# Attention and a low-rank mixer on one core: first batch reordered, two groups' turn of u moved to transfers, bias rows issued one head earlier

## The chip, the cores and the metric

The kernel runs on one core of a Trainium2 chip. The metric is device time in microseconds (us), from runs of the whole kernel; lower is better. A profiled execution gives a trace of every instruction of the five engines (PE is TensorE, DVE is VectorE, ACT is ScalarE, POOL is GpSimd, SP is SyncE) and of the DMA queues. PE's weight loads are a track of their own, PEld.

## What is computed

Two parts follow each other. The first is causal attention with a bias per position, for 8 batches of 8 heads, 576 positions and head size 64. The second takes the heads side by side as x (8 x 576 x 512), mixes the positions with a rank-32 product, and runs a feed-forward layer of width 2048.

```python
scores = scale * np.matmul(q, k.transpose(0, 1, 3, 2))
cum = np.cumsum(np.maximum(s, 0.0), axis=-1)
bias = -(cum[:, :, :, None] - cum[:, :, None, :])
scores = np.where(causal, -1e9, scores + np.minimum(bias, 0.0))
attn = softmax(scores)                       # along the last axis
x = (attn @ v).transpose(0, 2, 1, 3).reshape(B, S, H * D)
...
h = x.transpose(0, 2, 1) @ U @ V             # U: 576 x 32, V: 32 x 576
u = x + h.transpose(0, 2, 1)
out = u + np.maximum(u @ w_ch1, 0.0) @ w_ch2
```

## The kernel before

**Groups.** The batches go through in five groups, `GROUPS = [(0,), (1,), (2, 3), (4, 5), (6, 7)]` (L22). The first two groups share the activation tiles of one pair of batches: batch 0 is tiles 0 to 3, batch 1 tiles 5 to 8, and tile 4 (`TAIL`) holds the last 64 rows of both. A group of two batches has nine tiles of 128 rows (`TILES`, L24). The work of a group is its *front*, attention and then the mixer, and its *back*, the feed-forward layer.

**Front.** A pair of heads of one group has a number n, 0 to 19; n = 8 to 11 belong to group 2, 12 to 15 to group 3, 16 to 19 to group 4. For a head, `scores` (L455) multiplies keys by queries in four steps, each into a PSUM bank of tag "s" (three banks), and ACT writes exp of it to `pT` (L473). `weigh` (L501) multiplies these weights by v, which carries a column of ones for the sum, and DVE divides (L519, L523) into `x_sb`. Keys and queries must stand with the head dimension on the partitions. For groups 0 and 1 `turn_six` (L431) does that with six TensorE transposes and two copies of 64 x 576 (L451). For n from 8 on, POOL casts them to DRAM (`cast`, L190) and `turn_kq` (L208) brings them back with four transposing DMAs of SP's queue (L217), one per batch and tensor, 1152 rows of 128 each. Four extra rows per pair, 64 to 67 of `kT` and `qT`, hold the bias split into parts: `bias_rows` (L347) loads them from DRAM on SP's queue (L353). A transposing DMA writes all 128 partitions, so the bias rows of a pair have to wait until the transposes of that pair have landed. `kT` and `qT` have room for four pairs (`RING`). SP issues its DMAs in order, the outputs among them (L783, L787).

At the end of pair n of a front, `attention` issues on SP `bias_rows(n + 1)` for n above 10 and `turn_kq(n + 2)` for n above 9 (L639 to L642); for earlier pairs a table `late` does it (L634).

`mix` (L700) then forms `ux`, the product with U over all tiles (L708), copies it (L713), and for each tile multiplies by V (L736) and adds to x in place on DVE (L740). u must also stand with its 512 columns on the partitions, as `uT`, for the feed-forward layer. The inner function `turn` does that for two tiles at a time: eight TensorE transposes into a "pv" bank (L723) and one DVE copy (L728).

**Back.** `ffn` (L751) has two phases. In the first, for each stretch of columns in `CUTS` (L660; one stretch is a third of 1152 for the groups of two) and each of 16 slices of the width, four matmuls (L591) fill a bank "f" (three banks) and ACT takes the positive part to `hT` (L763). In the second, sixteen matmuls per tile (L768) are added to x on DVE (L779) into one of five buffers `o` and written out.

**Order of the work.** All is written out by hand. The loop at L804 runs the back of group g and steps the front of group g + 1 between its steps: both are generators that yield their cost in us, and the front is stepped as long as it is behind a ratio:

```python
ratio = FRONT[g + 1] / (BACK[g] - LEAD[g])
due, live = -LEAD[g] * ratio, True
...
due += cost * ratio
```

`LEAD[g]` is how much of the back runs before the front of the next group begins. With `FRONT` = 24.6 and `BACK` = 61.7 the front ends with the back.

**First batch.** It has no back to run beside. `first_attention` (L538) turns the keys and queries of the head pairs (`turns`, alternating keys and queries of pairs 0 to 3), runs the eight heads, and puts the weighing of a head and parts of batch 0's mixer and feed-forward between the scores. `ux_first` (L668) and `turn_first` (L678) are the mixer of batch 0; `turn_first` gets `uT` straight from a matmul with the identity plus the product with V. `begun` are three "s" banks with the first feed-forward products. `stir(n)` (L161) issues n matmuls of 128 x 128 whose result is not used.

Of the kernel before, what the change touches and what calls it, by code (L numbers as in the profile page):

```python
# [47 lines left out]
def kernel(  # L48
# [12 lines left out]
    nc = tc.nc  # L61
# [41 lines left out]
    uT = const([128, 4, 2 * S], BF16, "uT")  # L103
# [57 lines left out]
    def stir(n):  # L161


        ps = bank("pv", 2)
        for _ in range(n):
            nc.tensor.matmul(ps[:, :128], lhsT=stirrer, rhs=stirrer, start=True, stop=True)  # L166
# [261 lines left out]
        make_keep(0)  # L428


    def turn_six(g, hp, which, scalar=False):  # L431


        pb = (bank("f", 3) if g == 0 else bank("pv", 2)).bitcast(BF16)
        for hh in range(2):
            for t in range(SUB // 2):
                c = RP * (hh * (SUB // 2) + t)
                nc.tensor.transpose(
                    pb[:, c : c + RP],
                    six[g][which][:, 2 * hp + hh, 2 * D * t : 2 * D * t + 2 * D],  # L440
                    identity[:RP, :RP],
                )
        n = pairs.index((g, hp))
        to = (kT, qT)[which](n)[:D].rearrange(
            "d (h p t e) -> d h p t e", h=2, t=SUB // 2, e=2
        )
        for e in range(2):
            from_ = pb[64 * e : 64 * e + 64, : RP * SUB].rearrange(
                "d (h t p) -> d h p t", h=2, p=RP
            )  # L450
            (nc.scalar.copy if scalar else nc.vector.tensor_copy)(  # L451
                to[:, :, :, :, e], from_
            )

    def scores(kt_, qt_, p, c, tail0, first=False):  # L455

# [81 lines left out]
    def first_attention():  # L538


        turns = [(hp, which) for hp in range(4) for which in range(2)]
        for i, (hp, which) in enumerate(turns[:3]):
            turn_six(0, hp, which, scalar=i == 1)
            stir((3, 14, 34)[i])
        prepare_second()
        done, second = [], cumulate(1, 2)
        for h in range(H):
            n, hh = h // 2, h % 2
            p = next_p()
            if h == 2:  # L550
                next(second)
            quanta = scores(kT_all, qT_all, p, PW * n + S * hh, 448, True)
            next(quanta)
            next(quanta)
            if h == 7:
                ux_first((0, 1), nc.vector.tensor_copy)

            if h > 3:
                weigh(*done.pop(0))
            for _ in quanta:  # L560
                pass
            done.append((0, p, 0, h))
            if h in (3, 5, 6):
                next(second)
            if h + 3 < len(turns):
                turn_six(0, *turns[h + 3])
            if h < 5:
                stir((12, 12, 12, 12, 6)[h])
            if h == 7:
                turn_first((0, 1), 0, 256, nc.vector.tensor_copy)  # L570
            if h > 4:
                weigh(*done.pop(0))
        weigh(*done.pop(0))
        turn_first((0, 1), 256, 512, nc.scalar.copy)
        ux_first((2,), nc.vector.tensor_copy)
        begun = [bank("s", 3) for _ in range(3)]
        for nf in range(3):
            for kt in range(2):
                first_product(begun[nf], nf, kt, *CUTS[0][0])
        turn_first((2,), 0, 512, nc.scalar.copy)  # L580
        ux_first((3,), nc.vector.tensor_copy)
        for nf in range(3):
            first_product(begun[nf], nf, 2, *CUTS[0][0])
        turn_first((3,), 0, 256, nc.vector.tensor_copy)
        turn_first((3,), 256, 512, nc.scalar.copy)
        for _ in second:
            pass
        return begun
# [7 lines left out]
    def attention(g, side):  # L596

        pending = None
        turns = [(hp, which) for hp in range(4) for which in range(2)] if g == 1 else []


        for cost in (0.25, 1.8, 0.9) if turns else ():
            turn_six(g, *turns.pop(0))
            yield cost
        for hp in range(H // 2):
            n = pairs.index((g, hp))
            for hh in range(2):
                for i, bi in enumerate(SIDES[g]):
                    p = next_p()
                    quanta = scores(  # L610
                        kT_all, qT_all, p, place(n).start + (2 * i + hh) * S,
                        512 if bi == 0 else 448,
                    )
                    yield next(quanta)
                    yield next(quanta)
                    nc.vector.tensor_tensor(  # L616
                        p[:, D4:O1], p[:, D4:O1], keep[bi], ALU.min
                    )
                    if turns:
                        turn_six(g, *turns.pop(0))  # L620
                        yield 0.25
                    if pending is not None:
                        weigh(*pending)
                        yield 0.48
                    for cost in quanta:
                        yield cost
                    pending = (g, p, bi, 2 * hp + hh)
                    for _ in range(2):
                        next(side, None)
            if g == 1 and hp == 1:  # L630
                nc.vector.tensor_copy(x_sb[1][:64, TAIL, :], x_sb[0][:64, TAIL, :])


            late = {5: 8, 6: 9, 7: 10, 8: 11}  # L634
            if n - 1 in late:
                bias_rows(late[n - 1])
            if n in late:
                turn_kq(late[n])
            if n > 9:  # L639
                if n > 10:  # L640
                    bias_rows(n + 1)
                turn_kq(n + 2)  # L642
            if g == 2 and hp == 0:

                for t in (kT(11), qT(11)):
                    nc.gpsimd.tensor_copy(hold, t[:1, PW : PW + 1])
                load_group(g + 1)
            if g > 2 and hp == 1:

                c = (2 * hp) * D  # L650
                nc.gpsimd.tensor_copy(hold, x_sb[g % 2][:1, 0, c : c + 1])  # L651
                load_group(g + 1)
        weigh(*pending)
        yield 0.48
        for _ in side:
            pass
# [1 line left out]


    CUTS = [  # L660
        ((0, 256), (256, 512)),
        ((512, 832), (832, 1152)),
        *[((0, 384), (384, 768), (768, 1152))] * 3,
    ]
# [35 lines left out]
    def mix(g):  # L700

        x, tl = x_sb[g % 2], TILES[g]


        ux = bank("f", 3)
        for n, t in enumerate(tl):
            i = n % 2
            nc.tensor.matmul(  # L708
                ux[64 * i : 64 * i + 64, :], lhsT=U_cat[:, t, :64], rhs=x[:, t, :],
                start=(n == i), stop=(n + 2 >= len(tl)),  # L710
            )
        yield 0.13 * len(tl)
        nc.vector.tensor_copy(ux_sb, ux)  # L713
        if g == 1:

            nc.vector.tensor_copy(ux_sb[:32], ux0[:32])  # L716
        yield 0.65

        def turn(ns):
            pb = bank("pv", 2).bitcast(BF16).rearrange("p (d n c) -> p d n c", d=4, c=128)  # L720
            for m, n in enumerate(ns):
                for d in range(4):
                    nc.tensor.transpose(  # L723
                        pb[:, d, m, :], x[:, tl[n], 128 * d : 128 * d + 128], identity
                    )
            w = 128 * len(ns)
            c = 128 * tl[ns[0]]
            nc.vector.tensor_copy(  # L728
                uT[:, :, c : c + w],
                pb.rearrange("p d n c -> p d (n c)")[:, :, :w],  # L730
            )

        done = 0
        for n, t in enumerate(tl):
            hp_ = bank("f", 3)
            nc.tensor.matmul(  # L736
                hp_, lhsT=V_cat[:, t, :], rhs=ux_sb,
                start=True, stop=True,
            )
            nc.vector.tensor_add(x[:, t, :], x[:, t, :], hp_)  # L740
            yield 0.22
            if n >= 2 and n % 2 == 0:
                turn([done, done + 1])
                done += 2
                yield 0.45
        while done < len(tl):
            turn(list(range(done, min(done + 2, len(tl)))))
            done += 2
            yield 0.45

    def ffn(g, begun):  # L751

# [43 lines left out]

    LEAD = [5.0, 8.0, 0.0, 0.0]
    FRONT = [0.0, 17.3, 24.6, 24.6, 24.6]  # L800
    BACK = [27.4, 34.3, 61.7, 61.7, 61.7]

    begun = first_attention()
    for g in range(len(GROUPS)):  # L804
# [3 lines left out]
                pass  # L808
            break
        ahead = front(g + 1)  # L810
        ratio = FRONT[g + 1] / (BACK[g] - LEAD[g])
        due, live = -LEAD[g] * ratio, True
        for cost in back:
            due += cost * ratio
# [38 lines left out]
```

## Time and profile before

| | us |
|---|---|
| median of 3 runs | 389.03 (387.9 to 390.3) |
| the profiled execution, its own time | 388.87 |
| its span, first to last instruction | 387.2 |
| PE busy | 372.6 (96%) |
| PEld busy | 235.4 (61%) |
| ACT busy | 206.0 (53%) |
| DVE busy | 166.2 (43%) |
| POOL busy | 65.9 (17%) |

A group's line gives a duration from issue to the modelled end; matmuls overlap, so PE's cost of one is the distance between starts. "PEclk" is the clock that TensorE was granted, as a share of the full one. An instruction's line in the timeline gives in brackets how long its engine had been idle before it, and what ended that.

### The profile page before, as it was taken

What the parts mean: (1) busy time and instruction counts of PE and PEld (TensorE: products, weight loads), DVE (VectorE), ACT (ScalarE), POOL (GpSimd) and SP (SyncE); (2) the same over time, 40 slices, a digit from 0 to 9 for tenths busy, and PEclk for the clock granted to TensorE, in tenths of its full rate; (3) what the DMA queues carried; (4) which work ended last, traced back from release to release, by engine and by line L of the source; (5) the groups of instructions that cost most, each with busy time, mean ns of one, the idle gap of its engine ahead of it and who ended that gap; (6) DMA issues with size and microseconds to landing.
All of it is one profiled execution on the core that took longest, in us unless ns stands there. A gap on an engine that the chain in (4) does not pass through costs nothing.

```text
span 387.2 us, 8463 instructions
## 1 busy us (share of the span) xinstructions
PE 372.6 (96%) x3445; PEld 235.4 (61%) x3445; DVE 166.2 (43%) x385; ACT 206.0 (53%) x473; POOL 65.9 (17%) x104
## 2 busy tenths in 40 slices
PE   8899998999999979999999999999999999999995
PEld 8688865467766545666655456666655455655442
DVE  6484699551446581232243473332344471000221
ACT  4576865239977206888844007888744006773000
POOL 8784642100072200044300000000000000000000
PEclk9899999999999998999999999999999999999999
DMA  7999999999989999869991816800011110000122
GB/s 96 174 207 183 188 215 172 140 141 150 204 137 200 133 166 210 163 82 203 152 154 58 182 54 111 155 22 2 2 54 56 56 54 30 0 2 27 70 68 81
DMA packets 117989, 44.06 MB, mean 114 GB/s; under 512 B 99486, under 2 KB 113054, under 8 KB 117950
## 3 DMA queue, kind: packets, MB, share of 16 engines
q0 software_dynamic: 51376, 18.50, 44.4%
q1 hardware_dynamic: 66390, 24.99, 35.3%
q8 instruction: 27, 0.44, 0.5%
q14 instruction: 12, 0.10, 0.1%
q10 hardware_dynamic: 184, 0.03, 0.1%
HBM read 37.52 MB, written 16.97 MB: 141 GB/s over the span
## 4 chain that ended last, share of the span: by engine, by line
PE 83%; DMA 6%; DVE 5%; POOL 2%; ACT 1%; issue 1%; SPq 0%; POOLq 0%; ACTq 0%; DVEq 0%
PE ps_f L591 31%; PE ps_f L768 28%; PE ps_s L461 10%; PE ps_pv L513 8%; DMA qT<-kq_rows 3%; DMA hT<-in_k_dram 2%; PE ps_f L736 1%; PE ps_pv L723 1%; DVE qT L451 1%; DMA qT<-aug_rows 1%; POOL v_raw L229 1%; ACT pT L473 1%; POOL hT L203 1%; PE ps_f L708 1%; DVE kT L451 1%
## 5 line engine op out<-in xcount | busy, mean ns | idle before, releaser
L473 ACT ACTIVATE pT<-ps_s 128x448 bf16<-128x448 f32 (+1 forms) x256 | 120.5, 512 | 84.2 <-PE ps_s L461 81.7
L591 PE MATMUL ps_f<-uT,w 128*128 128x384 bf16 (+2 forms) x820 | 149.2, 316 | 0.0
L768 PE MATMUL ps_f<-w,hT 128*128 128x512 bf16 x576 | 147.5, 379 | 0.0
L763 ACT ACTIVATE hT<-ps_f 128x384 bf16<-128x384 f32 (+2 forms) x205 | 97.3, 476 | 54.8 <-PE ps_f L591 52.6
L591 PEld LDWEIGHTS <-w 128*128 128x128 bf16 x832 | 76.6, 98 | 35.3 <-issue 1.7
L461 PE MATMUL ps_s<-qT,kT 68*128 68x128 bf16 (+4 forms) x576 | 79.6, 242 | 4.6 <-DMA qT<-aug_rows 2.6
L768 PEld LDWEIGHTS <-hT 128*128 128x128 bf16 x576 | 52.1, 98 | 48.2 <-issue 2.4
L616 DVE TENSOR_TENSOR pT<-pT,keep 128x576 bf16<-128x576 bf16 x56 | 25.6, 456 | 108.5 <-ACT pT L473 108.2
L461 PEld LDWEIGHTS <-kT 68*128 68x128 bf16 x576 | 46.6, 98 | 35.8 <-issue 5.1
L779 DVE TENSOR_TENSOR o<-x_sb,ps_f 128x512 f32<-128x512 bf16 x36 | 24.6, 685 | 73.7 <-PE ps_f L768 71.9
L513 PEld LDWEIGHTS <-pT 128*128 128x128 bf16 x960 | 37.2, 97 | 11.7 <-DVE x_sb L528 1.7
L513 PE MATMUL ps_pv<-v_raw,pT 128*128 128x65 bf16 x960 | 40.8, 194 | 2.0 <-DVE qT L451 0.8
L229 POOL DMA_DIRECT2D v_raw<-in_v_dram x32 | 28.2, 891 | 32.6 <-PE ps_s L461 16.3
L523 DVE TENSOR_TENSOR x_sb<-ps_pv,rec 128x320 bf16<-128x320 f32 (+1 forms) x64 | 29.3, 458 | 2.2
L740 DVE TENSOR_TENSOR x_sb<-x_sb,ps_f 128x512 bf16<-128x512 bf16 x32 | 21.0, 685 | 4.7 <-PE ps_f L736 4.7
L651 POOL COPY hold<-x_sb 1x1 bf16<-1x1 bf16 x2 | 0.4, 178 | 100.4 <-DVE x_sb L523 100.4
L519 DVE RECIPROCAL rec<-ps_pv 128x5 f32<-128x5 f32 x64 | 12.2, 191 | 5.4 <-PE ps_pv L513 4.6
L166 PE MATMUL ps_pv<-hT 128*128 128x128 bf16 x141 | 12.1, 252 | 1.1 <-DVE hT L132 1.1
L728 DVE COPY uT<-ps_pv 128x1024 bf16<-128x1024 bf16 (+1 forms) x18 | 11.3, 630 | 4.3 <-PE ps_pv L723 4.0
L736 PE MATMUL ps_f<-ux_sb,V_cat 128*128 128x512 bf16 x32 | 11.8, 379 | 0.9 <-DVE ux_sb L716 0.4
L723 PEld LDWEIGHTS <-x_sb 128*128 128x128 bf16 x128 | 8.6, 98 | 5.2 <-issue 0.6
L166 PEld LDWEIGHTS <-hT 128*128 128x128 bf16 x141 | 10.5, 116 | 1.1 <-DVE hT L132 1.1
(88 smaller groups left out, 147.9 us busy)
## 6 DMA issues: line engine op xcount, KB each, us to landing
out_dram<-o SPq DMA_DIRECT2D x32, 256.0 KB
v_raw<-in_v_dram POOLq DMA_DIRECT2D x32, 128.0 KB, 17.9
w<-in_moe_w_ch_dram POOLq DMA_DIRECT2D x8, 512.0 KB, 12.5
kq_rows<-in_k_dram POOLq DMA_DIRECT2D x6, 576.0 KB, 11.1
kq_rows<-in_q_dram POOLq DMA_DIRECT2D x6, 576.0 KB, 14.5
out_dram<-o SPq DMA_DIRECT2D x8, 128.0 KB
hT<-in_k_dram POOLq DMA_DIRECT2D x4, 144.0 KB, 4.1
hT<-in_q_dram POOLq DMA_DIRECT2D x4, 144.0 KB, 4.9
```

The lines of the kernel that those rows point to most:

```text
L166: nc.tensor.matmul(ps[:, :128], lhsT=stirrer, rhs=stirrer, start=True, stop=True)
L229: nc.gpsimd.dma_start(out=dest[:, 5 * bi + t, :, :D], in_=v[b, :, 128 * t : 128 * t + 128].rearrange("h p d -> p h d"),)
L461: nc.tensor.matmul(ps[:, col : col + n], lhsT=kt_[:KA, c + kc : c + kc + 128], rhs=qt_[:KA, c + qc : c + qc + n], start=start, stop=stop,)
L473: nc.scalar.activation(p[:, at : at + n], ps[:, :n], EXP, scale=scale)
L513: nc.tensor.matmul(pv3[:, it, :], lhsT=p[:, at : at + 128], rhs=vr[:, TAIL if j == 4 else 5 * bi + j, h, :], start=(j == 0), stop=(j == it),)
L523: nc.vector.tensor_mul(x[:, 5 * bi : 5 * bi + n, h * D : h * D + D], pv3[:, :n, :D], rec[:, :n].unsqueeze(2).to_broadcast([128, n, D]),)
L591: nc.tensor.matmul(f1[:, : c1 - c0], lhsT=w1[:, kt, 128 * nf : 128 * nf + 128], rhs=uT[:, kt, c0:c1], start=(kt == 0), stop=(kt == 3),)
L616: nc.vector.tensor_tensor(p[:, D4:O1], p[:, D4:O1], keep[bi], ALU.min)
L740: nc.vector.tensor_add(x[:, t, :], x[:, t, :], hp_)
L763: nc.scalar.activation(hT[:, nf, c0:c1], f1[:, :cw], RELU)
L768: nc.tensor.matmul(f2, lhsT=hT[:, kt, 128 * t : 128 * t + 128], rhs=w2[:, kt, :], start=(kt == 0), stop=(kt == 15 and g > 0),)
L779: nc.vector.tensor_add(o, x_sb[g % 2][:, t, :], f2)
```

## The change

It has these parts.

- First batch: four turns instead of three go ahead of the heads, with 3, 14, 6 and 46 unused matmuls behind them instead of 3, 14 and 34. Within heads 0 to 4, three unused matmuls stand ahead of the third score step, and in heads 0 to 3 four more ahead of the last; the 12, 12, 12, 12 and 6 behind the heads are gone. The turns left stand behind heads 0, 1, 3 and 4 (before: 0 to 4); the last one is copied half by ACT and half by DVE. The first weighing moves from the middle of head 4 to its end.
- `CUTS[0]`: one stretch of 512 columns instead of two of 256. The three banks begun ahead of the feed-forward layer get their products with all 512 columns, three of four, before it starts.
- `turn` in `mix`, for groups 3 and 4: per tile one transposing DMA from `x_sb` to `uT` on SP's queue instead of TensorE transposes and a copy. Its cost in the interleaving is 0 instead of 0.45 per two tiles.
- `bias_rows(n + 1)` for n above 10 moves from the end of pair n to behind the first head of it.
- `LEAD` goes from 5, 8, 0, 0 to 5, 11, 8, 0, `FRONT` from 24.6 to 22.3 for groups 3 and 4, and a new `LAG` of 4.5 for the backs of groups 2 and 3 raises the ratio, so that the front of groups 3 and 4 is due to end 4.5 ahead of the back.

```diff
-    def turn_six(g, hp, which, scalar=False):
+    def turn_six(g, hp, which, by=(nc.vector.tensor_copy, nc.vector.tensor_copy)):
...
-            (nc.scalar.copy if scalar else nc.vector.tensor_copy)(
-                to[:, :, :, :, e], from_
-            )
+            by[e](to[:, :, :, :, e], from_)
...
-        for i, (hp, which) in enumerate(turns[:3]):
-            turn_six(0, hp, which, scalar=i == 1)
-            stir((3, 14, 34)[i])
+        for i, (hp, which) in enumerate(turns[:4]):
+            if i == 1:
+                turn_six(0, hp, which, (nc.scalar.copy, nc.scalar.copy))
+            else:
+                turn_six(0, hp, which)
+            stir((3, 14, 6, 46)[i])
         prepare_second()
...
-            if h == 2:
-                next(second)
             quanta = scores(kT_all, qT_all, p, PW * n + S * hh, 448, True)
             next(quanta)
             next(quanta)
             if h == 7:
                 ux_first((0, 1), nc.vector.tensor_copy)
 
+            if h > 4:
+                weigh(*done.pop(0))
+            else:
+                stir(3)
+            next(quanta)
+            if h < 4:
+                stir(4)
+            next(quanta)
+            done.append((0, p, 0, h))
+            if h in (2, 4, 6):
+                next(second)
+            if h < 2:
+                turn_six(0, *turns[h + 4])
+            elif h == 3:
+                turn_six(0, *turns[6])
+            elif h == 4:
+                turn_six(0, *turns[7], (nc.scalar.copy, nc.vector.tensor_copy))
             if h > 3:
                 weigh(*done.pop(0))
-            for _ in quanta:
-                pass
-            done.append((0, p, 0, h))
-            if h in (3, 5, 6):
-                next(second)
-            if h + 3 < len(turns):
-                turn_six(0, *turns[h + 3])
-            if h < 5:
-                stir((12, 12, 12, 12, 6)[h])
-            if h == 7:
-                turn_first((0, 1), 0, 256, nc.vector.tensor_copy)
-            if h > 4:
-                weigh(*done.pop(0))
+        turn_first((0, 1), 0, 256, nc.scalar.copy)
+        ux_first((2,), nc.vector.tensor_copy)
         weigh(*done.pop(0))
         turn_first((0, 1), 256, 512, nc.scalar.copy)
-        ux_first((2,), nc.vector.tensor_copy)
+        turn_first((2,), 0, 512, nc.scalar.copy)
         begun = [bank("s", 3) for _ in range(3)]
+
+        def begin(nf, kts, c0, c1):
+            for kt in kts:
+                nc.tensor.matmul(
+                    begun[nf][:, c0:c1], lhsT=w1[:, kt, 128 * nf : 128 * nf + 128],
+                    rhs=uT[:, kt, c0:c1], start=(kt == 0 and c0 == 0), stop=False,
+                )
+
         for nf in range(3):
-            for kt in range(2):
-                first_product(begun[nf], nf, kt, *CUTS[0][0])
-        turn_first((2,), 0, 512, nc.scalar.copy)
+            begin(nf, (0, 1), 0, 256)
         ux_first((3,), nc.vector.tensor_copy)
         for nf in range(3):
-            first_product(begun[nf], nf, 2, *CUTS[0][0])
+            begin(nf, (0, 1), 256, 512)
+        for nf in range(3):
+            begin(nf, (2,), 0, 512)
...
+                    if n > 10 and (hh, i) == (0, 0):
+                        bias_rows(n + 1)
...
             if n > 9:
-                if n > 10:
-                    bias_rows(n + 1)
                 turn_kq(n + 2)
...
-        ((0, 256), (256, 512)),
+        ((0, 512),),
...
         def turn(ns):
+
+            if g > 2:
+                for n in ns:
+                    c = 128 * tl[n]
+                    nc.sync.dma_start(
+                        out=uT[:, :, c : c + 128],
+                        in_=x[:, tl[n], :].rearrange("p (d c) -> p d c", c=128), transpose=True,
+                    )
+                return 0.0
...
+            return 0.45
...
-                turn([done, done + 1])
+                yield turn([done, done + 1])
                 done += 2
-                yield 0.45
...
-    LEAD = [5.0, 8.0, 0.0, 0.0]
-    FRONT = [0.0, 17.3, 24.6, 24.6, 24.6]
+    LEAD = [5.0, 11.0, 8.0, 0.0]
+    FRONT = [0.0, 17.3, 24.6, 22.3, 22.3]
...
+    LAG = [0.0, 0.0, 4.5, 4.5]
...
-        ratio = FRONT[g + 1] / (BACK[g] - LEAD[g])
+        ratio = FRONT[g + 1] / (BACK[g] - LEAD[g] - LAG[g])
```

More of the change, by code (lines that the diff above doesn't have):

```diff
@@ L742, in mix @@
             if n >= 2 and n % 2 == 0:
-                turn([done, done + 1])
+                yield turn([done, done + 1])
                 done += 2
-                yield 0.45
         while done < len(tl):
-            turn(list(range(done, min(done + 2, len(tl)))))
+            yield turn(list(range(done, min(done + 2, len(tl)))))
             done += 2
-            yield 0.45
     def ffn(g, begun):
```

## The prediction

> **What bounds the kernel.** I read the page first, then who waited for whom, then the timeline of PE and of SP's queue round the few places where PE was idle.
>
> ```profile
> PE   8899998999999979999999999999999999999995
> ...
> PEclk9899999999999998999999999999999999999999
> ```
>
> In 40 slices of 9.7 us, PE is at nine tenths or more nearly everywhere (96% of the span). From about 30 us on, what shortens the kernel is either work taken off PE or one of the few places where PE waits or runs at a lower clock. Of these, one is large:
>
> ```profile
> 146.00 0.21 PEld L461 LDWEIGHTS <-kT 68*128 68x128 bf16 x4 [3.00 <-DMA kT<-aug_rows]
> 146.03 0.36 PE L461 MATMUL ps_s<-qT,kT 68*128 68x64 bf16 x4 [2.64 <-DMA qT<-aug_rows]
> ```
>
> ```profile
> 143.30:146.00 2.70, 0.09 (x1) 0.00 (x0) 0.82 (x2) 0.00 (x0) 0.00 (x0) 1.00 1.55 143
> 146.00:150.00 4.00, 3.97 (x19) 2.24 (x20) 0.46 (x1) 2.54 (x6) 0.00 (x0) 0.57 1.11 251
> 150.00:154.00 4.00, 4.00 (x44) 2.73 (x42) 1.11 (x3) 3.36 (x8) 0.00 (x0) 1.00 0.95 220
> ```
>
> The second fence is busy time by stage (span, PE, PEld, DVE, ACT, POOL, then the clock). The first scores of pair 12 wait 2.64 us for its bias rows, and the 4 us behind the wait run at a mean clock of 0.57. Why the rows are late stands in SP's timeline:
>
> ```profile
> 131.06 3.56 SPq L217 DMA_TRANSPOSE qT<-kq_rows  x1
> 134.71 1.07 SPq L787 DMA_DIRECT2D out_dram<-o  x2
> 138.88 0.27 SPq L353 DMA_DIRECT2D kT<-aug_rows  x1
> 141.76 0.25 SPq L353 DMA_DIRECT2D qT<-aug_rows  x1
> 142.07 1.24 SPq L217 DMA_TRANSPOSE kT<-kq_rows  x1
> 143.36 2.37 SPq L217 DMA_TRANSPOSE qT<-kq_rows  x1
> 145.77 1.35 SPq L217 DMA_TRANSPOSE kT<-kq_rows  x1
> 147.16 1.39 SPq L217 DMA_TRANSPOSE qT<-kq_rows  x1
> ```
>
> Pair 12's last transpose is issued at 131.06; the four below the rows are pair 13's, with less traffic. The chain of waits has (start, us):
>
> ```profile
> 131.06 10.65 DMA qT<-kq_rows
> ...
> 141.76 4.13 DMA qT<-aug_rows
> ```
>
> So 10.65 us to land, then 4.13 us for the row that waited for it, to 145.9.
>
> **The change part by part.** I sum on the profiled execution: 388.87 us, a span of 387.2 and 1.67 around it. The median is 0.16 more, which I add at the end.
>
> *u of groups 3 and 4.* Each group loses 9 tiles of 4 transposes:
>
> ```profile
> 214.00:235.00 21.00, 2.83 (x36) 2.43 (x36) 1.00 0.43 106
> 300.00:321.00 21.00, 2.83 (x36) 2.43 (x36) 1.00 0.15 51
> ```
>
> (L723 alone: PE, PEld, clock, DMA share.) Eight in a row took 0.61 us and one lasts 0.219, so starts stand (0.61 - 0.22) / 7 = 56 ns apart. 72 x 0.056 = 4.0 us off PE, which has other work on both sides in these stretches (21.00 busy of 21.00). The bound above is 2 x 2.83 = 5.7; I take 4.0, since the ends overlap with the next matmuls. The 10 DVE copies (630 ns) were not what PE waited for.
>
> Added on SP are 9 DMAs per group. No transpose out of SBUF is in the trace; the nearest rows are L217's. One moves 1152 rows of 256 B in 1.24 to 1.39 us of issue when the queue is free; a tile is 512 such rows, so 0.6 us, 5.4 us for nine. The worst L217 issue is 5.22 us, beside a cast: 2.3 us per tile, 21 us for nine. Landing: pair 13's last issue ends at 148.55 and the query bias row that waits for it leaves at 150.46, so 1.9 us more. When is a tile needed? The next back begins with columns 0 to 383, three tiles. The new front costs 22.5 by its own yields and runs at 22.3 / 57.2 = 0.39 of the back, so it ends 4 us of back before it; the nine tiles' adds come 0.22 / 0.39 + 0.22 = 0.78 us apart, so tile 2 is issued some 9 us ahead. At 0.6 us it has landed with 6 us to spare, at 2.3 us it lands at about 9 us after the first add, still ahead of 11; tiles 3 to 5 have a stretch of 64 matmuls (10.4 us) more. Cost 0 either way. Behind them on SP stand outputs (five buffers, one filled every 5 us or so) and pair 17's and 18's loads, due tens of us later. The price if this cover fails is the second rival's.
>
> The Trainium skill speaks against this part: VectorE: DVE Perf Modes, "The three transpose paths", has 390 ns for a 128 x 128 block on TensorE and 1309 ns by DMA, and its rules advise TensorE where PSUM will do; an estimate by its figure is 36 x 1.309 = 47 us of transfer per group. The trace does not agree for blocks in a stream: L217 does nine in 1.3 us, and TensorE one every 56 ns.
>
> With the turns gone the adds (L740, 5.95 us for nine, 0.66 each) come closer: every 0.22 / 0.453 + 0.22 = 0.70 us in group 3. With L779's share (0.685 per 3.5 us of back) DVE needs 0.76. Nine tiles: +0.5 us (0 to 1).
>
> *Bias rows and LEAD.* The front of group 3 now starts after 8 us of back, and pair 12's rows leave SP as soon as its transposes have landed, ahead of later outputs. Those transposes are paced by the casts (POOL, issued from 109.38 once pair 11 has landed), which no part of the change moves. So the rows land near 146, and are needed at 142.9 + 8 = 151: 5 us of cover. Saved: 2.64 + 4.0 x (1 - 0.57) = 2.64 + 1.7 = 4.35 us; 0 to 4.35, taken whole because of that cover. Each earlier `bias_rows` blocks SP until the next pair's transposes land, at worst 10.65 us as here; queued behind it are outputs, for which five buffers last some 25 us. Casts of group 4 wait for head 2 of pair 13's x, which comes some 5 us of back later; pair 16 needs them only at 235 (before: landed by 195).
>
> LEAD 11 makes the front of group 2 denser, 24.6 / 23.3 = 1.056 per us of back against 24.6 / 26.3 = 0.935. There ACT is as full as PE:
>
> ```profile
> 92.00:100.00 8.00, 7.86 (x106) 6.04 (x104) 3.65 (x11) 7.92 (x22) 0.00 (x0) 1.00 1.21 182
> ```
>
> The stretch with relu beside exp is 17.4 - 11 = 6.4 us of back, and takes 0.12 x 6.4 = 0.8 us more front. If ACT alone set the pace that would be 1 us; I take +0.3 (0 to 1).
>
> *First batch.* What it waits for is the last keys:
>
> ```profile
> 17.50 1.69 ACT L473 ACTIVATE pT<-ps_s 128x448 bf16<-128x448 f32 x4 [1.17 <-PE ps_s L461]
> ...
> 21.08 0.43 PE L438 MATMUL ps_f<-identity,hT 96*128 96x96 bf16 x6 [0.39 <-DMA hT<-in_k_dram]
> ```
>
> Nothing moves that transfer, so all ahead of 21.05 gains nothing. Behind it, PE has work without a real pause to the back's start at 35.04. There 18 unused matmuls (12 + 6, about 60 ns) become 3: -0.9 us. The split copy frees queries 0.8 us sooner, but weighings fill PE meanwhile. Against it: four heads at ACT's 1.69 to 1.75 us from 11.8 on end at about 18.8, so PE now idles 2.3 us before 21.05. Both low-clock stretches of the trace follow idle time: a mean of 0.54 in 13.6 to 16.9 behind 1.26 us, and the one above behind 2.64. A third would cost up to 1.7 us, some of it beside ACT, so 1.3. I take 0 for the whole (-0.9 to +1.4). The Trainium skill (TensorE: Matmul & The Clock Gate, "What's actually happening") has the activity window run freely, 3413 ns long; by that the wait may fall in one window or be cut in two, and the sum would be 1.3 more or the same by chance. The trace agrees as to the length: 4.0 us at a mean of 0.57 are 3.4 us at half.
>
> The 512 columns cost PE the same (4.58 us for 42 of 256 is 109 ns; 512 at 0.43 us per two is 215). Nine products of 0.11 us move ahead into waits of 0.40 and 0.29 us; the fourth product then waits for ACT's copy of the last 256 columns, about 0.2 later. Zero.
>
> **Sum:** 388.87 - 4.0 - 4.35 + 0.5 + 0.3 + 0 = 381.3; with the 0.16, 381.4. By the bounds of the parts other than the stall: down to 381.4 - 0.8 - 0.9 - 1.7 = 378.0, up to 381.4 + 0.5 + 0.7 + 1.4 = 384.0.
>
> **The rivals.** *The stall stays or moves.* The rows come after 151 because the transposes land later in a queue that is already full (DMA share 1.6), or group 3's start waits for something else as long. For it: 10.65 us of landing shows how loaded the queues are. Against: 5 us of cover. 381.4 + 4.35 = 385.8, little changed. Chance 0.10.
>
> *Transposes out of SBUF are slow, and the kernel gets slower.* Place: the start of the backs of groups 3 and 4, L591 waiting for uT. Tile 2 must land within 11 us of the first add, so it decides from (11 - 1.9) / 3 = 3 us per tile on. At 4.07 us, which L217 takes for its 1152 rows at 126.94 beside a cast, tile 2 lands at 14.1 (3.1 late), and tile 8 at 38.5, against 11 + 3.1 + 20.8 = 34.9 (3.6 late): 6.7 us a group, 381.4 + 13.4 = 394.8. For it: source and size are new, and each row goes alone (256 B). Against: L217's slow rows lie beside casts and loads of v, and none of these runs at 300 to 321 (DMA share 0.15). Chance 0.08. By the Trainium skill's figure (VectorE: DVE Perf Modes, as above) a tile would take 5.2 us, and the same working gives about 416, an estimate.
>
> **How the numbers follow.** The forecast has 0.81, the rivals 0.10 and 0.08, and 0.01 is left. A measurement of this kernel tells about 1%, 3.9 us, from no change. The forecast's whole range lies under 385.1, so faster 0.81; the first rival is within 1%, with a little for mixtures: 0.11; slower 0.08. The range reaches from the lower bound to the first rival: 378.0 to 386.0.
>
> **What would show it.** L723 down from 128 to 56 matmuls, L728 from 18 to 8. No idle of PE over 1 us behind 30 us, and a clock of 1.00 at 140 to 155. The first L591 of groups 3 and 4 with no wait on a transfer; the new SP transposes near 0.6 us each. The first batch's back starting within 34 to 36.5. A wait of PE on uT's transfers, or a bias row still ending PE's idle time, would prove me wrong, as would a low clock that does not come back after 21.

## The result and the profile after

The changed kernel takes 383.74 us (median of 4 runs, 383.26 to 384.49), the kernel before in the same comparison 388.55. The ratio is 0.9871, with a 95% interval of 0.9833 to 0.9909. Its profiled execution took 384.49 us with a span of 382.8, 4.4 less than before. Forecast were 381.4 us, so the direction held, and 2.3 us of the gain are missing.

The page's first line of busy time and the two lines of the slices that were shown of before:

```profile
PE 367.0 (96%) x3310; PEld 224.7 (59%) x3310; DVE 158.9 (42%) x373; ACT 205.6 (54%) x459; POOL 65.7 (17%) x104
...
PE   7889997989999999999999999999999999999995
...
PEclk9989999999999999999999999999999999999999
```

The dent near 145 us is gone from both rows; a new one stands in the seventh slice, 57 to 67 us. PE was busy 372.6 us and is busy 367.0, 5.6 less; the span gave 4.4. So some idle time is new. The list of who waited for whom has PE's two largest waits, neither of which is among the waits of before in this size (us in total, times, longest):

```profile
PE ps_f L438 <- DMA hT<-in_k_dram: 3.2, 2, 2.9
...
PE ps_pv L511 <- DVE qT L451: 1.9, 1, 1.9
```

The first is the wait for the last keys of batch 0 and was foreseen at 2.3 us. The second was not foreseen. Busy time by stage (stretch, its length, PE, PEld, DVE, ACT, POOL, granted clock, DMA share, GB/s), round the first and round the second:

```profile
17.60:20.40 2.80, 0.03 (x1) 0.03 (x2) 0.46 (x2) 0.65 (x2) 2.01 (x5) 1.00 1.48 201
20.40:24.50 4.10, 4.10 (x49) 3.51 (x50) 1.97 (x3) 2.64 (x5) 3.94 (x9) 0.58 1.23 205
...
63.00:65.20 2.20, 0.28 (x9) 0.24 (x9) 2.10 (x6) 0.68 (x2) 0.00 (x0) 1.00 2.13 161
65.20:69.00 3.80, 3.80 (x29) 1.92 (x25) 2.06 (x6) 0.82 (x2) 1.56 (x2) 0.55 2.00 143
```

Each wait is followed by some 4 us at a little over half the clock. In the third row DVE is the engine at work (2.10 of 2.20).

The clearest account is where the same matmul stands in the two traces. The timeline of PE gives the start of each back, by its first product into an "f" bank (L591 before, L606 after):

| from the span's start, us | before | after | stage before | stage after | difference |
|---|---|---|---|---|---|
| back of group 0 | 35.36 | 36.46 | 35.36 | 36.46 | +1.10 |
| back of group 1 | 81.83 | 84.80 | 46.47 | 48.34 | +1.87 |
| back of group 2 | 142.90 | 146.84 | 61.07 | 62.04 | +0.97 |
| back of group 3 | 234.00 | 231.75 | 91.10 | 84.91 | -6.19 |
| back of group 4 | 320.63 | 316.38 | 86.63 | 84.63 | -2.00 |
| end of the span | 387.15 | 382.78 | 66.52 | 66.40 | -0.12 |

The stage of group 2's back got 6.2 us shorter: the stall at 143 us with its low clock, and one group's transposes. The stage of group 3's back got shorter by just one group's transposes, 2.0. The first rows hold the loss. The first batch now does 1.3 us of feed-forward products more (nine products of 0.109 us, and three fourth products of 0.216 instead of 0.109), so its 1.10 are no loss; but the stage after it, which has those 1.3 us less to do, got 1.87 longer instead of 1.3 shorter. That is 3.2 us. Some 1.2 of it is the low clock: in the run with unused matmuls below, the same stage ran at full clock behind the same wait and took 47.14 us instead of 48.34. The stage with LEAD 11, that of group 1's back, got 1.0 longer.

### The profile page after: what moved, and what is told of

The parts are those of the page before. It is cut to its first block, busy times and chain, and to the rows that moved or that the text cites. A ratio compares the mean times of both kernels' runs of the same rounds, so it can differ in the third digit from the quotient of the medians.

```text
span 382.8 us, 8201 instructions
## 1 busy us (share of the span) xinstructions
PE 367.0 (96%) x3310; PEld 224.7 (59%) x3310; DVE 158.9 (42%) x373; ACT 205.6 (54%) x459; POOL 65.7 (17%) x104
## 4 chain that ended last, share of the span: by engine, by line
PE 85%; DVE 7%; POOL 2%; DMA 2%; issue 1%; ACT 1%; POOLq 0%; ACTq 0%; DVEq 0%
PE ps_f L606 32%; PE ps_f L791 30%; PE ps_s L459 10%; PE ps_pv L511 8%; DMA hT<-in_k_dram 2%; DVE x_sb L765 2%; PE ps_f L761 1%; PE ps_f L723 1%; POOL v_raw L229 1%; POOL hT L203 1%; DVE qT L451 1%; DVE kT L451 1%; ACT pT L471 1%; DVE o L802 1%; PE ps_pv L747 1%
## 5 line engine op out<-in xcount | busy, mean ns | idle before, releaser
L471 ACT ACTIVATE pT<-ps_s 128x448 bf16<-128x448 f32 (+1 forms) x256 | 119.3, 513 | 68.2 <-PE ps_s L459 66.5
L606 PE MATMUL ps_f<-uT,w 128*128 128x384 bf16 (+2 forms) x756 | 142.4, 325 | 0.8 <-DVE uT L752 0.8
L786 ACT ACTIVATE hT<-ps_f 128x384 bf16<-128x384 f32 (+2 forms) x189 | 93.9, 497 | 66.6 <-PE ps_f L606 64.0
L606 PEld LDWEIGHTS <-w 128*128 128x128 bf16 x759 | 69.9, 98 | 39.0 <-issue 1.1
L526 DVE TENSOR_SCALAR x_sb<-ps_pv,rec 64x64 bf16<-64x64 f32 x32 | 9.3, 291 | 0.5
L451 DVE COPY kT<-ps_f 64x576 bf16<-64x576 bf16 x8 | 6.4, 798 | 5.0 <-PE ps_f L438 5.0
```

What stands on the lines that cost most here:

```text
L471: nc.scalar.activation(p[:, at : at + n], ps[:, :n], EXP, scale=scale)
L606: nc.tensor.matmul(f1[:, : c1 - c0], lhsT=w1[:, kt, 128 * nf : 128 * nf + 128], rhs=uT[:, kt, c0:c1], start=(kt == 0), stop=(kt == 3),)
L786: nc.scalar.activation(hT[:, nf, c0:c1], f1[:, :cw], RELU)
```

## The experiments

All times are medians of 6 runs (12 where said), beside runs of the kernel before on the same chip. "Less" and "more" without another name are against the changed kernel's 383.74. The changed kernel wasn't run again beside them; the kernel before had medians of 388.53 to 389.09 there, against 388.55 above. The 95% interval of a ratio of 6 runs reaches some 0.5% (1.9 us) to each side. So a difference of about 1 us between two medians is weak by itself, and the starts in the traces have to carry it.

### What the loss between 36 and 85 us comes from

**The first batch as before.** `first_attention`, `turn_six` and `CUTS[0]` are those of the kernel before, all else is changed.

```diff
-        ((0, 512),),
+        ((0, 256), (256, 512)),
...
-        for i, (hp, which) in enumerate(turns[:4]):
+        for i, (hp, which) in enumerate(turns[:3]):
+            turn_six(0, hp, which, scalar=i == 1)
+            stir((3, 14, 34)[i])
```

> The first batch, its columns (two stretches of 256) and the products begun ahead are those of the kernel before; all else is the changed kernel. Theory A: the new first batch costs 3 us, because the front of batch 1 is set by DVE from 46 to 65 us and the earlier feed-forward tile puts its add in front of DVE's copies of queries. Then PE's wait of 1.92 us at 63 us and the low clock behind it go, the feed-forward layer of batch 1 begins near 82 us instead of 84.8, and the time is about 381 (380 to 382). Theory B: the new first batch gains its unused matmuls as such, and the loss comes from elsewhere: 383.7 or more.

Measured: 381.32 us (380.71 to 382.98), ratio 0.9829 [0.9784, 0.9874]. Group 1's back begins at 81.62 us, 46.75 behind group 0's. Theory A holds in time and place: 2.4 us less. It leaves open which of the two parts of the new first batch costs.

**The columns as before, the new order of heads kept.**

```diff
-        for nf in range(3):
-            begin(nf, (0, 1), 0, 256)
+        for nf in range(3):
+            for kt in range(2):
+                first_product(begun[nf], nf, kt, *CUTS[0][0])
         ux_first((3,), nc.vector.tensor_copy)
         for nf in range(3):
-            begin(nf, (0, 1), 256, 512)
-        for nf in range(3):
-            begin(nf, (2,), 0, 512)
+            first_product(begun[nf], nf, 2, *CUTS[0][0])
```

(with `CUTS[0]` as above)

> Two stretches of 256 columns and the products begun ahead as in the kernel before; the new order of heads stays. Theory A: it is the columns and the 1.3 us of products moved ahead that shift the back against batch 1's front and put the first tile's add ahead of DVE's copies; so the wait at 63 us is near 0.5 us again, and the time is that of the kernel with the whole first batch as before, 381.3 (380.7 to 382). Theory B: the new order of heads is what costs: 383.5 or more.

Measured: 381.98 us (380.84 to 383.57), ratio 0.9858 [0.9811, 0.9906]. The stage is 46.75 us again, the same as with the whole first batch of before, and PE's wait at 64 us is 0.58. So it is the columns, and the products moved ahead with them. The 0.7 us against the run before may be the price of the new order of heads, as this profile too has a low clock behind the wait for the keys and the other has none; but the two intervals overlap, so it isn't shown.

Why the columns matter shows on DVE. The timeline of DVE, first of the kernel before, then of the changed one (start, us, what):

```profile
61.69 0.28 DVE L631 COPY x_sb<-x_sb 64x512 bf16<-64x512 bf16 x1
61.89 0.44 DVE L616 TENSOR_TENSOR pT<-pT,keep 128x576 bf16<-128x576 bf16 x1
62.36 1.63 DVE L451 COPY qT<-ps_pv 64x576 bf16<-64x576 bf16 x2
64.02 0.20 DVE L519 RECIPROCAL rec<-ps_pv 128x5 f32<-128x5 f32 x1
...
65.01 0.69 DVE L779 TENSOR_TENSOR o<-x_sb,ps_f 128x512 f32<-128x512 bf16 x1
```

```profile
62.02 0.28 DVE L648 COPY x_sb<-x_sb 64x512 bf16<-64x512 bf16 x1
62.32 0.69 DVE L802 TENSOR_TENSOR o<-x_sb,ps_f 128x512 f32<-128x512 bf16 x1
62.93 0.45 DVE L631 TENSOR_TENSOR pT<-pT,keep 128x576 bf16<-128x576 bf16 x1
63.30 1.61 DVE L451 COPY qT<-ps_pv 64x576 bf16<-64x576 bf16 x2
64.94 0.20 DVE L517 RECIPROCAL rec<-ps_pv 128x5 f32<-128x5 f32 x1
```

DVE has no pause in either. The weighing behind these copies needs the bank that they read. With 1.3 us less of back ahead of it, the first output tile's add stands in front of the last copies of queries instead of behind them, and PE arrives at the weighing sooner: it waits from 63.05 to 64.97 instead of 0.57 us.

A second wait on DVE goes with the columns, at the end of the stage. The first products of group 1's back, before and after (how many a line holds depends on the stretch asked for):

```profile
81.83 0.84 PE L591 MATMUL ps_f<-uT,w 128*128 128x320 bf16 x5
...
84.80 1.38 PE L606 MATMUL ps_f<-uT,w 128*128 128x320 bf16 x9 [0.80 <-DVE uT L752]
```

These 0.80 us stand in every profile with the 512 columns and in none with two stretches of 256. Two further runs vary the order on DVE and its load.

**Batch 1's front 1 us of back earlier.**

```diff
-    LEAD = [5.0, 11.0, 8.0, 0.0]
+    LEAD = [4.0, 11.0, 8.0, 0.0]
```

> LEAD of the back of group 0 is 4 instead of 5: batch 1's front begins 1 us of back earlier. Theory A: what makes the stage from 36 to 85 us longer is the order on DVE: the add of the first output tile stands ahead of the last copies of batch 1's queries. With the front 1 us earlier it stands behind some or all of them, the wait of 1.92 us shrinks to 0.5 and the low clock goes: 381 to 382. Theory B: the order doesn't matter and DVE's chain as such sets the stage, so it gains the 1 us of earlier start at most: 382.7 to 383.7.

Measured: 382.37 us (381.49 to 382.76), ratio 0.9862 [0.9815, 0.9909]; 1.4 less. DVE's timeline of this run has the add behind the copies:

```profile
62.48 1.62 DVE L451 COPY qT<-ps_pv 64x576 bf16<-64x576 bf16 x2
64.14 0.69 DVE L802 TENSOR_TENSOR o<-x_sb,ps_f 128x512 f32<-128x512 bf16 x1
```

PE still waits 1.31 us there, not 0.5. The wait is shorter by 0.6 us, about one DVE add, so the order is part of it, and the larger part of the wait stays without it. What the order is worth in time isn't shown: the stage is 47.13 us here, with the clock full, and the run with unused matmuls below has 47.14 at full clock with the order as in the changed kernel. The time lies between the ranges of the two theories and settles neither.

**Batch 1's copies shared between ACT and DVE.**

```diff
                     if turns:
-                        turn_six(g, *turns.pop(0))
+                        turn_six(g, *turns.pop(0), (nc.scalar.copy, nc.vector.tensor_copy))
```

> Batch 1's turns inside the heads are copied half by ACT and half by DVE; all else is the changed kernel. Theory A: DVE sets the front of batch 1 from 46 to 65 us, so that five copies of 0.8 us less on it take PE's wait of 1.92 us at 63 us and the low clock behind it away: 380 to 381.5. Theory B: the copies only change engines, ACT's exps come later by as much, and PE waits for the weights instead: 383 to 385.

Measured: 380.87 us (379.65 to 382.03), ratio 0.9826 [0.9779, 0.9873]; 2.9 less. The stage is 44.91 us, shorter than before the change. DVE's timeline at the same place:

```profile
60.00 0.69 DVE L802 TENSOR_TENSOR o<-x_sb,ps_f 128x512 f32<-128x512 bf16 x1
60.60 0.45 DVE L631 TENSOR_TENSOR pT<-pT,keep 128x576 bf16<-128x576 bf16 x1
61.08 0.80 DVE L451 COPY qT<-ps_pv 64x576 bf16<-64x576 bf16 x1
61.92 0.20 DVE L517 RECIPROCAL rec<-ps_pv 128x5 f32<-128x5 f32 x1
```

The add is in front here too, but there is one copy of 0.80 behind it instead of two, and PE's wait is 0.44 us. ACT took the other halves without a price that shows. The time and the wait are those of theory A: DVE sets the front of batch 1. The 1.3 us of products moved out of the stage are still not given back, though. With the copies shared and the columns of before (the last run below), the stage holds these products and takes 44.50 us.

### The wait for the keys and the clock

**Unused matmuls in the wait.**

```diff
             elif h == 3:
+                stir(48)
                 turn_six(0, *turns[6])
```

> 48 unused matmuls (2.7 us) fill PE's wait of 2.85 us ahead of the turn of the last keys. Theory A: the wait is what drops the clock in some runs (0.58 from 20.4 to 24.5 us in the changed kernel's profile); with it filled the clock stays at 1.00 there, and the time falls by at most the 1.3 us that the low stretch costs behind the keys: 382.4 to 383.7. Theory B: by the runs with idle waits of 1.7 us and no drop, the drop is a matter of chance and rare: 383.7, or up to 0.5 more where the keys land before the 48 are through.

Measured: 382.86 us (382.54 to 384.11), ratio 0.9881 [0.9838, 0.9925]; 0.9 less. The stages of this run at the place of the first two rows above:

```profile
17.60:20.40 2.80, 2.74 (x51) 2.57 (x48) 0.98 (x2) 0.61 (x2) 1.72 (x5) 1.00 1.32 205
20.40:24.50 4.10, 3.77 (x71) 3.12 (x69) 2.61 (x4) 3.42 (x8) 3.94 (x9) 1.00 1.24 207
```

PE is busy and the clock is full. 71 matmuls instead of 49 fit into the same 4.1 us. That is theory A as far as the clock goes. But the 0.9 us aren't the price of this stretch alone, since the second low stretch is missing here too. In this profile the back of group 0 starts 0.67 us earlier than in the changed kernel's (35.79), and the stage behind it is 1.20 shorter with its wait of 1.92 us unchanged. The mean clock was 1.00 in five of the six runs and 0.99 in all four of the changed kernel. Why the second stretch stayed away isn't shown.

### The transposes, LEAD and the bias rows

**u turned by TensorE again.** The branch for groups 3 and 4 is off, FRONT is 24.6 and LAG 0.

```diff
-            if g > 2:
+            if False:
...
-    FRONT = [0.0, 17.3, 24.6, 22.3, 22.3]
+    FRONT = [0.0, 17.3, 24.6, 24.6, 24.6]
-    LAG = [0.0, 0.0, 4.5, 4.5]
+    LAG = [0.0, 0.0, 0.0, 0.0]
```

> u of groups 3 and 4 is turned by TensorE again, with FRONT 24.6 and LAG 0 for them; all else is the changed kernel. Theory A: the transfers take 72 matmuls of 56 ns off a full PE, 2.0 us in each of the two stages, and nothing waits for them: 383.7 + 4.0 = 387.7. Theory B: the end of the front, 4.5 us ahead of the back, is what saves the time, or the adds on DVE eat part of it: 384.5 to 386.5.

Measured: 388.00 us (12 runs, 386.11 to 389.09), ratio 0.9985 [0.9955, 1.0015]; 4.3 more. Theory A, to 0.3 us. In the profile the stages of the backs of groups 2 and 3 take 86.64 and 86.63 us, 1.73 and 2.00 more than in the changed kernel's.

**LEAD of group 1's back at 8.**

```diff
-    LEAD = [5.0, 11.0, 8.0, 0.0]
+    LEAD = [5.0, 8.0, 8.0, 0.0]
```

> LEAD of the back of group 1 is 8 instead of 11. Theory A: the denser front of group 2 costs 1 us beside ACT and at the mixer's end, so 382.7. Theory B: the stage from 85 to 147 us is 1 us longer for another reason (transfers, or a front that started later), and the time stays at 383.7; or group 3's bias rows come earlier relative to the need and it is a little faster or slower by under 0.4.

Measured: 382.92 us (381.81 to 384.27), ratio 0.9876 [0.9827, 0.9924]; 0.8 less. The stage is 61.08 us, within 0.01 that of the kernel before and of every other profile with LEAD 8 there, and 62.04 in every profile with LEAD 11, whatever the first batch. So the 1.0 us belongs to LEAD 11. It is not in one wait of PE; what theory A names as its cause isn't shown.

**Bias rows at the end of the pair again, LEAD as changed.**

```diff
-                    if n > 10 and (hh, i) == (0, 0):
-                        bias_rows(n + 1)
...
             if n > 9:
+                if n > 10:
+                    bias_rows(n + 1)
                 turn_kq(n + 2)
```

> The bias rows leave at the end of a pair again; LEAD stays at 5, 11, 8, 0. Theory A: the 8 us of back ahead of group 3's front are what removed the stall at 143 us; the earlier issue adds nothing, because SP waited for the transposes anyway: 383.7 within 0.5. Theory B: the rows' place on the queue is needed too: the stall comes back in part, 385 to 388.

Measured: 395.13 us (393.66 to 396.39), ratio 1.0180 [1.0132, 1.0227]; 11.4 more, beyond both theories. Pair 12's scores wait for no bias rows, as theory A has it. But PE waits for bias rows 3.87 us at 200 and 3.03 us at 288. PE's timeline, then SP's, at the first:

```profile
200.27 0.28 PE L459 MATMUL ps_s<-qT,kT 68*128 68x192 bf16 x2
204.41 0.53 PE L459 MATMUL ps_s<-qT,kT 68*128 68x64 bf16 x4 [3.87 <-DMA qT<-aug_rows]
```

```profile
196.64 4.28 SPq L810 DMA_DIRECT2D out_dram<-o  x2
201.03 0.27 SPq L353 DMA_DIRECT2D kT<-aug_rows  x1
201.41 0.34 SPq L353 DMA_DIRECT2D qT<-aug_rows  x1
```

The rows stand behind two outputs on SP's queue, and the second of them leaves only when PE has finished that tile. With LEAD 8 the pairs lie so far into the back's second phase that outputs are ahead of the rows. The wait at 288 us is of the same kind, one output ahead of the rows (287.40 and 287.87), but it lies in group 3's back, whose LEAD is 0 as in the kernel before. There the new FRONT and LAG are what moved the pairs: 22.3 / 57.2 = 0.390 of the back instead of 24.6 / 61.7 = 0.399. The two stages are 5.45 and 3.20 us longer than in the changed kernel's profile. Issued a head earlier, the rows stand in front of the outputs. So the new LEAD, FRONT and LAG are usable only with the early issue.

**LEAD of group 2's back, on a ground without the losses.** Two kernels have the first batch and columns of the kernel before; the first has LEAD 5, 8, 8, 0, the second 5, 8, 0, 0.

```diff
-    LEAD = [5.0, 8.0, 8.0, 0.0]
+    LEAD = [5.0, 8.0, 0.0, 0.0]
```

> First batch and columns of the kernel before, and LEAD 5, 8, 8, 0; all else as changed. It is the ground for the next run. Theory A: the two gains add, 381.3 - 0.8 = 380.5 (379.8 to 381.2). Theory B: LEAD 11 costs nothing by itself, and the 0.8 seen alone was scatter: 381.3.

> The same with LEAD 5, 8, 0, 0: group 3's front starts with the back again, as in the kernel before, but its bias rows leave a head earlier. Theory A: the rows land near 146 us whenever they are issued, since SP waits for the transposes; so PE waits again near 143 us, 1.5 to 3 us and the low clock behind it: 382.5 to 385. Theory B: the earlier place on the queue is enough to bring the rows in time: 380 to 381.

Measured: 379.58 us (378.87 to 382.11), ratio 0.9765 [0.9714, 0.9816], for the first. 4.2 us came out, more than the sum of the two gains (2.4 and 0.8) and below theory A's range; in its profile the first batch is 1.2 us shorter than in the run with the first batch as before, which the edit of LEAD doesn't touch. For the second 380.91 us (379.90 to 384.06), ratio 0.9811 [0.9754, 0.9868]. In its profile PE waits 0.36 us at the place of the 2.64 of before (PE's timeline, then the chain of waits):

```profile
142.83 0.36 PE L461 MATMUL ps_s<-qT,kT 68*128 68x64 bf16 x4 [0.36 <-DMA qT<-aug_rows]
```

```profile
129.07 11.51 DMA qT<-kq_rows
...
140.63 2.06 DMA qT<-aug_rows
```

The transposes land no faster than before (11.51 us against 10.65), and the row leaves hardly earlier against the need: 1.35 us ahead of the back's first product (141.98) instead of 1.14. But it takes 2.06 us instead of 4.13. Two outputs that stood ahead of the rows on SP's queue before (issued at 134.71) stand behind them here (140.98), and the DMA share from 139 to 142 us is 0.56 instead of 1.59. That is theory B as far as this execution goes, and it fits the place on the queue; the loads of v also end some 2 us earlier here (last issue at 129.86 instead of 132.03), which no run separates. Two of its six runs stand at 383.68 and 384.06 us with a mean clock of 0.99, against 379.9 to 381 in the others; whether the wait is back in those wasn't profiled. LEAD 8 against 0 is 1.3 us by the medians, with ranges that overlap, but only 0.25 in the stage that it sets (84.90 against 85.15); the profiles differ by another 0.76 before that stage begins.

### Putting it together

Two kernels join what helped. The first is the changed kernel with the shared copies, LEAD 5, 8, 8, 0 and the 48 unused matmuls:

> The changed kernel with batch 1's copies split between ACT and DVE, LEAD 5, 8, 8, 0, and 48 unused matmuls in the wait for the last keys. Theory A: the gains of the three alone (2.9, 0.8, 0.9) add up since they lie in different stages: 379.1 (378.5 to 380). Theory B: they overlap, as the low clock is counted in more than one: 380 to 381.

The second has the first batch and columns of the kernel before, the shared copies and LEAD 5, 8, 8, 0:

> First batch and columns of the kernel before, batch 1's copies split between ACT and DVE, LEAD 5, 8, 8, 0. Theory A: with DVE relieved the order of the first tile's add no longer matters, so the old first batch gains nothing over the new one: 379.5 (379 to 380.5), level with the run of the same call on the new first batch. Theory B: the old first batch is better by itself, about 1 us: 378 to 379.

Measured: 379.39 us (379.28 to 381.20), ratio 0.9769 [0.9716, 0.9823], and 377.99 us (377.59 to 382.08), ratio 0.9739 [0.9682, 0.9795]. The gains add up in the first (4.35 of 4.6). The second is 1.4 us better by the medians, though two of its six runs (379.54 and 382.08) lie in or above the first one's range: theory B, and the lowest median here, 5.75 us below the changed one. The profiles say where: the back of group 0 starts at 36.36 us in the first and at 34.39 in the second, and the stage behind it takes 44.40 and 44.50. So with the products moved ahead the first batch is longer (the order of heads and the unused matmuls differ too), and the next stage is only 0.1 shorter. Of the change, the transfers and the early bias rows are worth keeping, LEAD 8 of group 2's back is worth little with them, and LEAD 11 and the new first batch with its columns aren't worth keeping.

## Why the prediction was right, point by point

*u of groups 3 and 4: right.* 4.0 us were forecast; the stage of group 3's back gave 2.00, and taking the part back cost 4.3. No product of groups 3 and 4 waited for uT. The cover was needed, though: SP took twice what was worked out. The line of these DMAs in the list of what writes uT (ns: least, median, most):

```profile
L739 SPq DMA_TRANSPOSE uT<-x_sb x18: 1207/1220/2219, 222.5 to 318.0; - x18
```

A tile's transpose holds SP for 1.22 us, not 0.6: its 512 rows take about as long to issue as the 1152 of L217 (1.24 to 1.39). The last one leaves at 318.05, after group 4's back has begun at 316.38, and is still in time, because only tiles 0 to 2 are needed then. The rival of slow transposes priced this form from 3 us per tile on, and 1.2 is far from it. The figure of the Trainium skill (VectorE: DVE Perf Modes, "The three transpose paths"), 1309 ns for one 128 x 128 block by DMA, isn't the cost of a block in this stream. Seven tiles of four blocks each leave SP in 9.11 us from 310.15 on, 1.3 us a tile; how long one alone takes to land isn't shown.

*DVE's adds without the turns, +0.5: half of it at most.* The term stood for group 3's front, which runs in the stage of group 2's back. There, taking the transposes back cost 1.73 us instead of 2.00, so 0.27 is what the adds can have cost. The stage of group 3's back fell by the full 2.00.

*Bias rows and LEAD 8, -4.35: right in size.* Group 2's stage fell by 6.19, which less 2.0 for the transposes is 4.2; with the transposes back on TensorE it is 86.64, 4.46 less than before. The reason was incomplete. I gave the whole of it to the 8 us of cover and counted the earlier issue only as something that may block the outputs. The run with late rows shows the reverse order to be the danger: rows behind outputs that wait for PE, 11.4 us. And in the run with LEAD 0 the wait is 0.36 us without any of that cover, in the one execution that was profiled. So in the profiled executions either part alone took this stall away, and with the rows issued early the 8 us are worth 0.25 in their stage.

*LEAD 11, +0.3: undersized.* It cost 0.97 us in the profile and 0.8 in the medians; the upper bound of 1 held it.

*The first batch's order, 0: right on balance.* The wait was forecast at 2.3 us and was 2.85, and the clock fell behind it as described. In the profile of the run that filled the wait, the back of group 0 starts 0.67 us earlier; its 0.9 in the medians holds the second low stretch too. That the sum came near 0 is partly luck. In the profiles with 512 columns and the wait unfilled, the back of group 0 starts anywhere from 35.28 to 38.25 us.

*The 512 columns, "Zero": this is the term that was mis-sized.* It measured 3.2 us in the profile (+1.87 where 1.3 less work stood), 1.2 of them low clock, and 1.8 in the medians of the run that takes the columns back alone (2.4 where the order of heads goes back too). I costed the columns by PE's time alone and looked at the back, which PE sets. The same stage runs batch 1's front, and there the chain of waits of before had DVE's copies (L451) in it from 46 to 64 us. Work taken out of such a stage on PE makes PE wait longer, and it shifts the order in which both generators hand work to DVE. Nor did I have a line for a second low clock; the bounds of the parts went to 384.0, so 383.74 lies at their edge. (The sum as written gives 381.5, not 381.4.)

*Rivals.* Neither of the two came. What did come, a wait of PE on DVE between 36 and 85 us, stood in neither. It did break a sign that I had named, no idle of PE over 1 us behind 30 us, as the 1.22 us broke that of 0.6 per transpose. The other signs came: 56 transposes and 8 copies are left, and the clock is 1.00 from 140 to 155 us.

## What to carry to other kernels

Before moving work from one stage into another, ask of both stages which engine sets them: the chain of waits showed DVE there, and a microsecond of PE's work taken out of it was paid for in the first batch and not given back. When a ratio or a start between two interleaved streams is changed, walk through every in-order queue again and see what has moved in front of what; a small load behind an output holds PE until that output has left (3.87 and 3.03 us here). Where a gain is smaller than forecast, the starts of the same instruction in both traces, stage by stage, find the stage at once.

## What the runs showed of the hardware

A wait of the same length may or may not drop TensorE's clock. In the run with the 48 unused matmuls PE waits for the same copies for 1.92 us, from 62.75 to 64.67, and the stage behind it reads:

```profile
62.70:64.70 2.00, 0.08 (x2) 0.04 (x2) 1.94 (x5) 0.68 (x2) 0.00 (x0) 1.00 2.18 168
64.70:68.50 3.80, 3.75 (x48) 2.46 (x50) 3.08 (x9) 1.69 (x4) 1.56 (x2) 1.00 2.16 138
```

48 matmuls at full clock, against 29 in the changed kernel's 3.80 us at 0.55. The wait of 3.03 us at 288 us in the run with late bias rows left the clock at 1.00 too (291 to 295 us), while the 1.26 us of the kernel before were followed by 0.54. In the lowest stretch of 4 us the mean is 0.50 (22 to 26 us, u turned by TensorE again), so I take half for the low clock. The Trainium skill (TensorE: Matmul & The Clock Gate, "What's actually happening") has a window of 3413 ns that isn't tied to the work. The traces agree as to the length: the low stretches come to 4.10 x 0.42 x 2 = 3.4 us and 3.80 x 0.45 x 2 = 3.4 us at half clock. By that rule part of what a wait costs would be a matter of where it falls, which no run here shows. A low stretch of 3.4 us at half is 1.7 us of matmul work, and the profile without the two of them was shorter by 0.67 and 1.20 us at their places.

A transposing DMA holds SP's queue for 1.22 us with 512 rows out of SBUF (median of 18), and with 1152 rows out of DRAM for 1.24 to 1.39 us in three of the four rows of pair 13; the longest of all L217 was 5.22 us.
